# Putting the two attention products of a window back to back, with three PSUM pairs in rotation

## The chip, the cores and the metric

One core of one Trainium2 chip. The metric is the device time of one execution in microseconds (us). TensorE is called PE below, VectorE DVE, ScalarE ACT. The profiled span is about 1.8 us shorter than the device time of the same execution (284.3 against 286.09 us for the kernel before), so spans are compared with spans and times with times. The granted clock is the share of full speed at which PE was clocked. The batches of runs were on different chips, with the kernel before beside them each time.

## The reference, cut to what matters

```python
kv  = np.einsum('bhsd,bhse->bhde', k, v)          # batch 8, heads 8, seq 576, dim 64
out = np.einsum('bhsd,bhde->bhse', q, kv)
rms = np.sqrt(np.mean(out * out, axis=-1, keepdims=True) + 1e-06)
x   = (out / rms * g_norm)                         # -> 4608 tokens x 512
h   = x @ w_in                                     # 512 -> 2048
g   = np.where(h > 0.0, h, np.exp(np.minimum(h, 0.0)) - 1.0)
y   = g @ w_out                                    # 2048 -> 512
```

The 4608 tokens go in nine groups T of 512. A batch has 576 tokens, so some groups cross a batch boundary.

## The kernel before

Groups 2 to 8 run in "windows". Window T does the two layers of group T on PE, and beside it the attention of group T + 1. PSUM has eight banks of 512 floats. Pairs A and B (two banks each) take turns for the first layer, two single banks hold the output sums, and one spare pair serves the attention, one product at a time.

```python
def at_tile():
    return ps_at.tile([P, 2, 512], FP32, name="at", tag="at")
...
def se(h):                                  # half h of the attention of group T
    def product():
        st["se", h] = at_tile()
        se_mm(T, h, st["se", h])            # 16 or 24 small matmuls
        sq = attp.tile([P, 2, DM], BF16, name="sq", tag="sq")
        nc.scalar.activation(sq, st["se", h], AF.Square)
        ...
    def sums():   # DVE: ss = sum of sq over 64
    def inv():    # ACT: Ln, then Exp with scale -0.5
    def scale():  # DVE: xs = se * ss out of PSUM: frees the pair; then a DMA transpose to xT
    def gain():   # DVE: xT *= g
...
for T in range(2, NT):
    ...
    early = {2: ("sum0", "inv0"), 4: ("sum1", "inv1"), 5: ("gain0",), 7: ("gain1",)}
    late = {0: ("kv",), 1: ("se0",), 2: ("mul0",), 3: ("se1",), 4: ("mul1", "ahead")}
    ...
    halves = {1: 5, 3: 6, 5: 7} if T == 2 else {0: 1, 1: 3, 2: 4, 3: 5, 4: 6, 5: 7}
```

`early` and `late` say at which of the eight first-layer steps a piece stands, ahead of that step's DVE part or behind it; `halves` places the second layer. `kv` is K^T V of one batch, 72 small matmuls; `ahead` turns the next q by DMA and then loads the following batch. In the traces the matmuls, ACT and DVE go through their instructions in the order written. The first-layer steps have an ELU behind them: ACT takes the exponential, DVE reads the pair again and frees it.

Of the kernel before, what the change touches and what calls it, by code (L numbers as in the profile page):

```python
# [16 lines left out]
def kernel(  # L17
# [105 lines left out]
            out=w_out_sb[:, fs, :], in_=moe_w_out.rearrange("(c p) f -> p c f", p=P)[:, fs, :]  # L123
        )

    def at_tile():
        return ps_at.tile([P, 2, 512], FP32, name="at", tag="at")

    def single(tag, name):
        pool = ps_x if tag == "x" else ps_m2  # L130
        return pool.tile([P, 512], FP32, name=name, tag=tag)

    def pair(tag, name):
        if tag in ("x", "m", "mx"):
            return [single(t, name) for t in (tag + tag)[:2]]
        return ps_m1.tile([P, 2, 512], FP32, name=name, tag=tag)

    def as_bf16(ps):
# [12 lines left out]
    def kv_mm(b, kv_ps, u, ls=range(2)):  # L151
        for j in range(RK):
            for s in range(2):
                rows = slice(s * 64, s * 64 + 64)
                for l in ls:
                    nc.tensor.matmul(  # L156
                        kv_ps[s][l * 64 : l * 64 + 64, u * 64 : u * 64 + 64],
                        lhsT=bf["k", b][rows, 2 * l + u, j, :],
                        rhs=bf["v", b][rows, 2 * l + u, j, :],
                        start=(j == 0),  # L160
                        stop=(j == RK - 1),
                    )
# [78 lines left out]
    def se_mm(T, h, se_ps):  # L241

        for i in range(2):
            (b0, j0), (b1, j1) = (slot_of(T, 4 * h + 2 * i + t) for t in range(2))
            parts = [(0, P, b0, j0, 2)] if b0 == b1 else [(0, 64, b0, j0, 1), (64, P, b1, j1, 1)]
            for m in range(4):
                u, s = m // 2, m % 2
                for l in range(2):
                    for lo, hi, b, j, n in parts:
                        nc.tensor.matmul(  # L250
                            se_ps[lo:hi, l, (4 * i + m) * 64 : (4 * i + m) * 64 + 64],
                            lhsT=qT[b][l * 64 : l * 64 + 64, s, u, j : j + n, :],
                            rhs=kv_of(b, l, u, s),
                            start=True,
                            stop=True,
                        )

    def attention(T):

        st = {}  # L260

        def kv():
            if T == B:
                return
            kv_ps = at_tile()
            for u in range(2):
                kv_mm(T, [kv_ps[:, s, :] for s in range(2)], u)
            nc.scalar.copy(
                kv_sb[:, T], kv_ps[:, :, 0:P].rearrange("p s (u e) -> p u s e", u=2)
            )  # L270

        def se(h):
            def product():
                st["se", h] = at_tile()
                se_mm(T, h, st["se", h])
                sq = attp.tile([P, 2, DM], BF16, name="sq", tag="sq")
                nc.scalar.activation(sq, st["se", h], AF.Square)  # L277
                st["sq", h] = sq

            def sums():  # L280
                ss = attp.tile([P, 2 * H], FP32, name="ss", tag="ss")
                st["ss", h] = ss
                nc.vector.reduce_sum(  # L283
                    out=ss,
                    in_=st.pop(("sq", h)).rearrange("p l (m e) -> p (l m) e", e=D),
                    axis=AX.X,
                )

            def inv():
                ss = st["ss", h]  # L290
                nc.scalar.activation(ss, ss, AF.Ln, bias=eps_col, scale=1.0 / D)
                nc.scalar.activation(ss, ss, AF.Exp, scale=-0.5)  # L292

            def scale():
                if h == 0:
                    st["xs"] = attp.tile([P, J, DM], BF16, name="xs", tag="xs")
                    x_tile(T)
                se_ps, ss = st.pop(("se", h)), st.pop(("ss", h))
                nc.vector.tensor_tensor(  # L299
                    out=st["xs"][:, 2 * h : 2 * h + 2, :].rearrange("p i (l m e) -> p l i m e", l=2, e=D),  # L300
                    in0=se_ps.rearrange("p l (i m e) -> p l i m e", i=2, e=D),
                    in1=ss.rearrange("p (l i m) -> p l i m", l=2, i=2).unsqueeze(4).to_broadcast([P, 2, 2, 4, D]),
                    op=ALU.mult,
                )
                for i in (2 * h, 2 * h + 1):
                    nc.sync.dma_start_transpose(
                        out=xT[T][:, :, i * P : i * P + P], in_=st["xs"][:, i, :]
                    )

            def gain():  # L310
                cols = slice(2 * h * P, 2 * h * P + 2 * P)
                nc.vector.tensor_scalar(  # L312
                    out=xT[T][:, :, cols],
                    in0=xT[T][:, :, cols],
                    scalar1=g_col,
                    scalar2=None,
                    op0=ALU.mult,
                )

            return product, sums, inv, scale, gain  # L320

        pieces = {"kv": kv}
        for h in range(2):
            for name, piece in zip(("se", "sum", "inv", "mul", "gain"), se(h)):
                pieces[f"{name}{h}"] = piece
        return pieces

# [62 lines left out]
    def mm1(T, i, tag, relu=False):  # L390
        if i == 0:
            g_tile(T)
        ps = pair(tag, "h_ps")
        mm1_part(T, i, ps, range(KC))
        return elu(T, i, ps, relu)
# [55 lines left out]
    def mm2_half(T, i):  # L451
        mm2(T, i // 2, 8 * (i % 2), 8 * (i % 2) + 8)
# [252 lines left out]
    for i, tag in enumerate("mBAmBAm"):  # L705
        if i < 4:
            mm1(1, i, tag)()
        else:
            freed[i], rest[i] = mm1(1, i, tag, "later")
        if i == 3:  # L710
            at["kv"]()
        if i == 4:
            at["se0"]()
            freed[4]()
            at["sum0"]()
            at["inv0"]()
        if i == 5:
            at["mul0"]()
            freed[5]()
        if i == 6:  # L720
            rest[4]()
            rest[5]()
    ps = pair("B", "h_ps")
    mm1_part(1, 7, ps, range(KC))
    at["se1"]()
    freed[7], rest[7] = elu(1, 7, ps, "later")
    at["sum1"]()
    at["inv1"]()
# [22 lines left out]



    def window(T, at, early, late, second, relu=(), opened=()):
        for i in range(8):
            if i < len(opened):
                mm1_part(T, i, opened[i], range(KC), slice(256, 512))
                rest = elu(T, i, opened[i], False)
            else:
                rest = mm1(T, i, "BA"[i % 2], i in relu)  # L760
            for name in early.get(i, ()):
                at[name]()
            if i in second:
                second[i]()
            rest()
            for name in late.get(i, ()):
                at[name]()

    for T in range(2, NT):
        at, early, late = {}, {}, {}  # L770
        if T + 1 < NT:
            at = attention(T + 1)
            if T + 2 < B:
                cast_q(T + 2)

                def ahead(b=T + 2):
                    turn_q(b)
                    if b + 1 < B:
                        after_turn(b)
                        fetch_ahead(b + 1)  # L780
                at["ahead"] = ahead
            else:
                at["ahead"] = lambda: None
            early = {2: ("sum0", "inv0"), 4: ("sum1", "inv1"), 5: ("gain0",), 7: ("gain1",)}
            late = {0: ("kv",), 1: ("se0",), 2: ("mul0",), 3: ("se1",), 4: ("mul1", "ahead")}
        if T == 2:
            early = {2: ("sum0", "inv0"), 5: ("sum1", "inv1", "mul1"), 6: ("gain0",), 7: ("gain1",)}
            late = {0: ("kv",), 1: ("se0",), 2: ("mul0",), 4: ("se1",), 5: ("ahead",)}
        halves = {1: 5, 3: 6, 5: 7} if T == 2 else {0: 1, 1: 3, 2: 4, 3: 5, 4: 6, 5: 7}
        second = {i: (lambda n=n: mm2_half(T - 1, n)) for i, n in halves.items()}  # L790
        if T > 2:
            window(T, at, early, late, second)
        else:
            g_tile(T)
            opened = [pair("B", "h_ps")]
            mm1_part(T, 0, opened[0], range(KC), slice(0, 256))
            window(T, at, early, late, second, (3, 5), opened)
        mm2_half(T, 0)
        mm2_half(T, 2)
    for i in (1, 3, 4, 5):  # L800
        mm2_half(NT - 1, i)
    last_columns()
# [30 lines left out]
```

## Time and profile before

| | before |
|---|---|
| device time, median (range) of 4 runs | 285.66 us (285.14 to 285.82) |
| span of the profiled run | 284.3 us |
| PE, DVE, ACT busy | 97%, 58%, 50% |
| blocks of small matmuls in the windows | 17 |

A busy PE of 97% does not by itself say that PE can go no faster, because ends of matmuls are modelled. What says it is the distance between starts: 216 ns for every dense matmul of 512 columns. Anything that makes a start-to-start distance longer than that is what can be saved, or lost.

### The profile page before, as it was taken

What the parts mean: (1) busy time and instruction counts of PE and PEld (TensorE: products, weight loads), DVE (VectorE), ACT (ScalarE), POOL (GpSimd) and SP (SyncE); (2) the same over time, 40 slices, a digit from 0 to 9 for tenths busy, and PEclk for the clock granted to TensorE, in tenths of its full rate; (3) what the DMA queues carried; (4) which work ended last, traced back from release to release, by engine and by line L of the source; (5) the groups of instructions that cost most, each with busy time, mean ns of one, the idle gap of its engine ahead of it and who ended that gap; (6) DMA issues with size and microseconds to landing.
All of it is one profiled execution on the core that took longest, in us unless ns stands there. A gap on an engine that the chain in (4) does not pass through costs nothing.

```text
span 284.3 us, 5120 instructions
## 1 busy us (share of the span) xinstructions
PE 274.6 (97%) x2089; PEld 129.1 (45%) x2123; DVE 164.8 (58%) x222; ACT 141.5 (50%) x209; POOL 49.9 (18%) x89
## 2 busy tenths in 40 slices
PE   7899999999899999999999999999999999999994
PEld 3434444444544444444444444444444444444443
DVE  3449532877567657754785378627863786344600
ACT  3778359594568255435542555345543554333311
POOL 7743303341034033032103210000000000000000
PEclk9999999999999999999999999999999999999999
DMA  7999999997999889679637971712150234020222
GB/s 209 193 204 206 205 260 240 202 246 113 184 273 145 165 204 226 83 173 264 149 37 173 256 165 34 157 37 74 39 111 0 74 39 111 0 76 0 74 74 75
DMA packets 50571, 39.46 MB, mean 139 GB/s; under 512 B 30964, under 2 KB 44020, under 8 KB 50548
## 3 DMA queue, kind: packets, MB, share of 16 engines
q0 software_dynamic: 15008, 21.30, 37.4%
q1 hardware_dynamic: 35136, 17.31, 29.5%
q10 hardware_dynamic: 404, 0.53, 0.5%
q8 instruction: 16, 0.26, 0.4%
q14 instruction: 7, 0.06, 0.1%
HBM read 36.70 MB, written 9.44 MB: 162 GB/s over the span
## 4 chain that ended last, share of the span: by engine, by line
PE 84%; DMA 7%; DVE 3%; SPq 2%; issue 1%; ACT 1%; POOL 0%; DVEq 0%; POOLq 0%
PE h_ps L382 39%; PE o_ps L403 39%; DMA w_in_sb<-in_moe_w_in_dram 3%; DMA v_bf<-in_v_dram 2%; DMA qT<-q_bf 2%; PE at L250 2%; PE at L156 1%; PE o_ps L440 1%; PE h_ps L569 1%; DVE xs L299 1%; DVE ss L283 1%; SPq L331 1%; DVE gT L366 1%; DVE elu_e L362 1%; PE qt_ps L174 0%
## 5 line engine op out<-in xcount | busy, mean ns | idle before, releaser
L403 PE MATMUL o_ps<-w_out_sb,gT 128*128 128x512 bf16 x548 | 128.5, 379 | 0.7 <-issue 0.2
L382 PE MATMUL h_ps<-xT,w_in_sb 128*128 128x512 bf16 (+1 forms) x540 | 126.4, 376 | 1.0
L350 ACT ACTIVATE elu_e<-h_ps 128x1024 bf16<-128x1024 f32 (+1 forms) x79 | 74.0, 952 | 89.6 <-PE h_ps L382 78.4
L403 PEld LDWEIGHTS <-gT 128*128 128x128 bf16 x560 | 54.3, 98 | 66.0 <-issue 0.9
L366 DVE TENSOR_TENSOR gT<-elu_e,h_ps 128x1024 bf16<-128x1024 bf16 (+1 forms) x67 | 77.2, 1157 | 6.9 <-PE h_ps L382 0.5
L382 PEld LDWEIGHTS <-w_in_sb 128*128 128x128 bf16 x560 | 53.2, 98 | 61.1 <-issue 0.2
L362 DVE TENSOR_SCALAR elu_e<-elu_e 128x1024 bf16<-128x1024 bf16 x72 | 31.4, 437 | 65.1 <-ACT elu_e L350 65.0
L419 ACT COPY o_sb<-o_ps 128x512 f32<-128x512 f32 x32 | 18.3, 587 | 20.8 <-PE o_ps L403 20.1
L103 POOL CAST q_bf<-st_q 128x384 bf16<-128x384 f32 x36 | 18.5, 557 | 37.6 <-DMA st_q<-in_q_dram 37.6
L283 DVE TENSOR_REDUCE ss<-sq 128x16 f32<-128x1024 bf16 x14 | 17.1, 1218 | 7.7 <-ACT sq L277 7.7
L299 DVE TENSOR_TENSOR xs<-at,ss 128x1024 bf16<-128x1024 f32 x14 | 17.1, 1219 | 1.9 <-ACT ss L292 1.9
L277 ACT ACTIVATE sq<-at 128x1024 bf16<-128x1024 f32 x14 | 14.4, 1029 | 1.1 <-PE at L250 1.1
L212 DVE SCALAR_TENSOR_TENSOR xT<-y_ps,g_col,rT 128x512 bf16<-128x512 f32 (+1 forms) x10 | 6.2, 641 | 10.2 <-ACT rT L209 7.9
L339 POOL COPY gate<-qT 1x16 bf16<-1x16 bf16 x5 | 1.1, 218 | 60.4 <-DMA qT<-q_bf 60.4
L355 ACT ACTIVATE elu_h<-h_ps 128x1024 bf16<-128x1024 f32 (+1 forms) x12 | 9.3, 817 | 0.0
L156 PEld LDWEIGHTS <-k_bf 64*64 64x64 bf16 x576 | 6.4, 107 | 5.4 <-issue 5.4
L90 POOL DMA_DIRECT2D v_bf<-in_v_dram x11 | 7.8, 708 | 4.2 <-DMA w_in_sb<-in_moe_w_in_dram 2.1
L90 POOL DMA_DIRECT2D k_bf<-in_k_dram x11 | 7.9, 718 | 3.1 <-DMA w_in_sb<-in_moe_w_in_dram 2.4
L312 DVE TENSOR_SCALAR xT<-xT,g_col 128x1024 bf16<-128x1024 bf16 x14 | 6.7, 480 | 1.9 <-DMA xT<-xs 1.9
L250 PEld LDWEIGHTS <-qT 64*128 64x128 bf16 (+1 forms) x248 | 4.5, 97 | 7.1 <-issue 5.9
L250 PE MATMUL at<-kv_sb,qT 64*128 64x64 bf16 (+1 forms) x248 | 6.5, 193 | 0.8 <-DMA qT<-q_bf 0.7
L366 DVE TENSOR_TENSOR gT<-elu_e,elu_h 128x1024 bf16<-128x1024 bf16 x9 | 6.5, 723 | 0.8
(57 smaller groups left out, 94.8 us busy)
## 6 DMA issues: line engine op xcount, KB each, us to landing
st_q<-in_q_dram POOLq DMA_DIRECT2D x6, 1152.0 KB, 8.1
out_dram<-o_sb SPq DMA_DIRECT2D x24, 256.0 KB, 3.4
k_bf<-in_k_dram POOLq DMA_DIRECT2D x6, 576.0 KB, 10.6
v_bf<-in_v_dram POOLq DMA_DIRECT2D x6, 576.0 KB, 13.3
out_dram<-o_sb SPq DMA_DIRECT2D x19, 128.0 KB, 2.4
w_out_sb<-in_moe_w_out_dram POOLq DMA_DIRECT2D x4, 512.0 KB, 15.0
w_in_sb<-in_moe_w_in_dram POOLq DMA_DIRECT2D x2, 512.0 KB, 11.2
q_bf<-in_q_dram POOLq DMA_DIRECT2D x3, 288.0 KB, 13.4
```

Of the source, the lines that this page charges most:

```text
L90: eng.dma_start(out=dst.rearrange("p m j d -> p m (j d)"), in_=in_[:, ms, :])
L103: nc.gpsimd.tensor_copy(out=bf["q", b][:, u, js], in_=raw[b][:, u::2, js, :].rearrange("p l j d -> p j l d"),)
L250: nc.tensor.matmul(se_ps[lo:hi, l, (4 * i + m) * 64 : (4 * i + m) * 64 + 64], lhsT=qT[b][l * 64 : l * 64 + 64, s, u, j : j + n, :], rhs=kv ...
L277: nc.scalar.activation(sq, st["se", h], AF.Square)
L283: nc.vector.reduce_sum(out=ss, in_=st.pop(("sq", h)).rearrange("p l (m e) -> p (l m) e", e=D), axis=AX.X,)
L299: nc.vector.tensor_tensor(out=st["xs"][:, 2 * h : 2 * h + 2, :].rearrange("p i (l m e) -> p l i m e", l=2, e=D), in0=se_ps.rearrange("p l ...
L350: nc.scalar.activation(e[:, lo:hi, :], h, AF.Exp)
L362: nc.vector.tensor_scalar(out=e, in0=e, scalar1=1.0, scalar2=1.0, op0=ALU.min, op1=ALU.subtract)
L366: nc.vector.tensor_tensor(out=gT[T][:, 2 * i + lo : 2 * i + hi, :], in0=e[:, lo:hi, :], in1=h, op=ALU.add if relu else ALU.max,)
L382: nc.tensor.matmul((ps[a] if isinstance(ps, list) else ps[:, a, :])[:, cols], lhsT=w_in_sb[:, c, f * P : f * P + P], rhs=xT[T][:, c, cols] ...
L403: nc.tensor.matmul(o_ps[T, j], lhsT=gT[T][:, f, j * P : j * P + P], rhs=w_out_sb[:, f, :], start=(f == 0), stop=(f == FC - 1),)
L419: nc.scalar.copy(o_sb[T, half][:, j % 2, :], o_ps[T, j])
```

## The change

The two products of group T + 1 stand back to back, in pairs C (the spare one) and B, and in two windows K^T V of a later batch follows at once in pair A. That leaves fewer places where PE goes from the dense 128 x 128 array to smaller tiles and back. All three pairs then rotate through the first layer. A window becomes a string of steps.

```diff
+        if tag == "C":
+            return ps_at.tile([P, 2, 512], FP32, name=name, tag="at")
...
+            elif kind == "X":
+                nxt["se0"]("C")
+                nxt["se1"]("B")
+                kv_out_ = kv_all(int(arg[0]), arg[1]) if arg else None
+                if kv_out_:
+                    kv_out_()
+                for name in ("sq0", "sq1", "sum0", "sum1", "inv0", "inv1"):
+                    nxt[name]()
+            elif step == "Y":
+                nxt["mul0"]()
+                nxt["mul1"]()
...
         if T == 2:
+            window(T, "M0B K3C E0 M1A H5 E1 M2B E2 R3A H6 E3 X Y H7 Q M4A E4 h0 R5C E5 M6A E6 G0 M7B G1 E7 h2")
+        elif T + 1 < NT:
+            first = "K%dC" % (T + 1) if T < 5 else ""
+            kv = "%dA" % (T + 2) if T in (4, 5) else ""
+            window(
+                T,
+                f"M0A {first} H1 E0 M1B H3 E1 M2A H4 E2 H5 X{kv} H6 Y Q M3A H7 E3 M4B E4 M5A E5 M6C E6 G0 M7B G1 E7 h0 h2",
+            )
```

M4B is first-layer step 4 into pair B (R: with the relu on ACT), E its DVE part, H and h an eighth of the second layer for the group before or this one, K K^T V, Q the `ahead` piece, G a gain.

More of the change, by code (lines that the diff above doesn't have):

```diff
@@ L124, in load_w_out @@
         )
-    def at_tile():
-        return ps_at.tile([P, 2, 512], FP32, name="at", tag="at")
     def single(tag, name):
@@ L256, in se_mm, with kv_all, product, square @@
                         )
+    def kv_all(b, tag):
+        kv_ps = pair(tag, "kv_ps")
+        for u in range(2):
+            kv_mm(b, [kv_ps[:, s, :] for s in range(2)], u)
+        return lambda: nc.scalar.copy(
+            kv_sb[:, b], kv_ps[:, :, 0:P].rearrange("p s (u e) -> p u s e", u=2)
+        )
     def attention(T):
         st = {}
-        def kv():
-            if T == B:
-                return
-            kv_ps = at_tile()
-            for u in range(2):
-                kv_mm(T, [kv_ps[:, s, :] for s in range(2)], u)
-            nc.scalar.copy(
-                kv_sb[:, T], kv_ps[:, :, 0:P].rearrange("p s (u e) -> p u s e", u=2)
-            )
         def se(h):
-            def product():
-                st["se", h] = at_tile()
+            def product(tag="C"):
+                st["se", h] = pair(tag, "se_ps")
                 se_mm(T, h, st["se", h])
+            def square():
                 sq = attp.tile([P, 2, DM], BF16, name="sq", tag="sq")
@@ L318, in gain @@
                 )
-            return product, sums, inv, scale, gain
-        pieces = {"kv": kv}
+            return product, square, sums, inv, scale, gain
+        pieces = {}
         for h in range(2):
-            for name, piece in zip(("se", "sum", "inv", "mul", "gain"), se(h)):
+            for name, piece in zip(("se", "sq", "sum", "inv", "mul", "gain"), se(h)):
                 pieces[f"{name}{h}"] = piece
@@ L710 @@
         if i == 3:
-            at["kv"]()
+            kv_all(2, "C")()
         if i == 4:
             at["se0"]()
+            at["sq0"]()
             freed[4]()
@@ L725 @@
     at["se1"]()
+    at["sq1"]()
     freed[7], rest[7] = elu(1, 7, ps, "later")
@@ L750 @@
     at["gain1"]()
-    def window(T, at, early, late, second, relu=(), opened=()):
-        for i in range(8):
-            if i < len(opened):
-                mm1_part(T, i, opened[i], range(KC), slice(256, 512))
-                rest = elu(T, i, opened[i], False)
-            else:
-                rest = mm1(T, i, "BA"[i % 2], i in relu)
-            for name in early.get(i, ()):
-                at[name]()
-            if i in second:
-                second[i]()
-            rest()
-            for name in late.get(i, ()):
-                at[name]()
@@ L769 @@
-    for T in range(2, NT):
-        at, early, late = {}, {}, {}
-        if T + 1 < NT:
-            at = attention(T + 1)
-            if T + 2 < B:
-                cast_q(T + 2)
-                def ahead(b=T + 2):
-                    turn_q(b)
-                    if b + 1 < B:
-                        after_turn(b)
-                        fetch_ahead(b + 1)
-                at["ahead"] = ahead
-            else:
-                at["ahead"] = lambda: None
-            early = {2: ("sum0", "inv0"), 4: ("sum1", "inv1"), 5: ("gain0",), 7: ("gain1",)}
-            late = {0: ("kv",), 1: ("se0",), 2: ("mul0",), 3: ("se1",), 4: ("mul1", "ahead")}
-        if T == 2:
-            early = {2: ("sum0", "inv0"), 5: ("sum1", "inv1", "mul1"), 6: ("gain0",), 7: ("gain1",)}
-            late = {0: ("kv",), 1: ("se0",), 2: ("mul0",), 4: ("se1",), 5: ("ahead",)}
-        halves = {1: 5, 3: 6, 5: 7} if T == 2 else {0: 1, 1: 3, 2: 4, 3: 5, 4: 6, 5: 7}
-        second = {i: (lambda n=n: mm2_half(T - 1, n)) for i, n in halves.items()}
-        if T > 2:
-            window(T, at, early, late, second)
-        else:
-            g_tile(T)
-            opened = [pair("B", "h_ps")]
-            mm1_part(T, 0, opened[0], range(KC), slice(0, 256))
-            window(T, at, early, late, second, (3, 5), opened)
-        mm2_half(T, 0)
-        mm2_half(T, 2)
@@ new lines, in mm1_rest, with window @@
+    def mm1_rest(T, i, tag, relu):
+        mm1_part(T, i, opened, range(KC), slice(256, 512))
+        return elu(T, i, opened, relu)
+    def window(T, steps):
+        rest = {}
+        nxt = attention(T + 1) if T + 1 < NT else None
+        for step in steps.split():
+            kind, arg = step[0], step[1:]
+            if kind in "MR":
+                i, tag = int(arg[0]), arg[1]
+                make = mm1_rest if T == 2 and i == 0 else mm1
+                rest[i] = make(T, i, tag, kind == "R")
+            elif kind == "E":
+                rest.pop(int(arg))()
+            elif kind == "H":
+                mm2_half(T - 1, int(arg))
+            elif kind == "h":
+                mm2_half(T, int(arg))
+            elif kind == "K":
+                kv_all(int(arg[0]), arg[1])()
+            elif kind == "X":
[9 more added lines that the diff above has]
+                nxt["mul1"]()
+            elif step == "Q":
+                b = T + 2
+                if b < B:
+                    turn_q(b)
+                if b + 1 < B:
+                    after_turn(b)
+                    fetch_ahead(b + 1)
+            elif kind == "G":
+                nxt[f"gain{arg}"]()
+            else:
+                raise ValueError(step)
@@ new lines @@
+    g_tile(2)
+    opened = pair("B", "h_ps")
+    mm1_part(2, 0, opened, range(KC), slice(0, 256))
+    for T in range(2, NT):
+        if T + 2 < B:
+            cast_q(T + 2)
+        if T == 2:
+            window(T, "M0B K3C E0 M1A H5 E1 M2B E2 R3A H6 E3 X Y H7 Q M4A E4 h0 R5C E5 M6A E6 G0 M7B G1 E7 h2")
[5 more added lines that the diff above has]
+                f"M0A {first} H1 E0 M1B H3 E1 M2A H4 E2 H5 X{kv} H6 Y Q M3A H7 E3 M4B E4 M5A E5 M6C E6 G0 M7B G1 E7 h0 h2",
+            )
+        else:
+            window(T, "M0A H1 E0 M1B H3 E1 M2A H4 E2 M3B H5 E3 M4A H6 E4 M5B H7 E5 M6A E6 M7B E7 h0 h2")
```

## The prediction

> **What bounds the kernel now.** I first read the page: the engine table, the groups, the chain of waits.
>
> ```profile
> PE 274.6 (97%) x2089; PEld 129.1 (45%) x2123; DVE 164.8 (58%) x222; ACT 141.5 (50%) x209; POOL 49.9 (18%) x89
> ...
> PE 84%; DMA 7%; DVE 3%; SPq 2%; issue 1%; ACT 1%; POOL 0%; DVEq 0%; POOLq 0%
> ...
> L403 PE MATMUL o_ps<-w_out_sb,gT 128*128 128x512 bf16 x548 | 128.5, 379 | 0.7 <-issue 0.2
> L382 PE MATMUL h_ps<-xT,w_in_sb 128*128 128x512 bf16 (+1 forms) x540 | 126.4, 376 | 1.0
> L283 DVE TENSOR_REDUCE ss<-sq 128x16 f32<-128x1024 bf16 x14 | 17.1, 1218 | 7.7 <-ACT sq L277 7.7
> L299 DVE TENSOR_TENSOR xs<-at,ss 128x1024 bf16<-128x1024 f32 x14 | 17.1, 1219 | 1.9 <-ACT ss L292 1.9
> L277 ACT ACTIVATE sq<-at 128x1024 bf16<-128x1024 f32 x14 | 14.4, 1029 | 1.1 <-PE at L250 1.1
> ```
>
> PE carries 84% of the chain and sits idle under 2 us before its two dense groups. DVE and ACT are half busy. So only two things can move the time: PE work that is not dense, and a new wait of PE. Next I read PE's timeline for one steady window (start, length, line):
>
> ```profile
> 102.19 1.89 PE L403 MATMUL o_ps<-w_out_sb,gT 128*128 128x512 bf16 x8
> 104.01 0.41 PE L250 MATMUL at<-kv_sb,qT 64*128 64x64 bf16 x16
> 104.35 1.90 PE L382 MATMUL h_ps<-xT,w_in_sb 128*128 128x512 bf16 x8
> 106.09 1.89 PE L403 MATMUL o_ps<-w_out_sb,gT 128*128 128x512 bf16 x8
> ```
>
> Dense groups of 8 start 1.73 us apart: 216 ns each, no slack. An attention product of 16 small matmuls stretches 102.19 to 104.35 to 2.16 us, so it costs 0.43. Single records split that: the last dense matmul starts at 103.700 and the first small one at 104.008, 308 ns instead of 216; the small ones go in pairs every 29 ns; from the last (104.229) to the next dense one is 122 ns. So about 0.1 us to enter and 0.11 to leave, besides 8 x 0.029 = 0.23 of work. A K^T V of 72 costs 0.80 by the same subtraction (128.764 to 129.783 less 0.216). A product with a group boundary in it uses two array shapes (64*128 and 64*64): 24 matmuls, 0.57, with another 125 ns step between the shapes.
>
> The waits of PE hold one more item, in the first later window:
>
> ```profile
> PE at L250 <- DMA qT<-q_bf: 0.7, 1, 0.7
> ```
>
> The records show two pauses there (77.05 to 77.36 and 77.36 to 78.26). From the last dense start (76.517) to the next (78.475) less 0.216 is 1.74 us where such a block costs 0.57: this wait costs 1.17 us.
>
> **What the Trainium skill says.** "TensorEngine Tiling (Array Packing)", Key Properties: changing the tiling mode, not just the tile, drains the TensorE. The trace agrees: 0.1 us at each change of shape. "TensorE: Matmul & The Clock Gate", the part on 56 against 53.3 ns: N / 2.4 + about 2.5 ns, 215.7 at N = 512; the trace has 216. "VectorE: DVE Perf Modes", the perf-mode tier table: a reduce runs at 1x, and a tensor_tensor with a PSUM operand at 1x. The trace agrees: 1218 and 1219 ns for 1024 elements. So four such DVE operations in a row cannot be quick, and that matters below.
>
> **The change part by part.** No instruction is added or removed on PE (4247 rows in both); the order alone changes. In a later window M, H, E are the first layer, half of a second-layer sum, and the DVE part of ELU; X is the two products back to back (into pairs C and B), with K^T V into A behind them in two windows; Y is the two scalings.
>
> (a) Fewer mode switches. Before: 17 blocks (5 K^T V, 12 products). Cost 5 x 0.80 + 9 x 0.44 + 3 x 0.57 = 9.7 us. After: 9 blocks, 3 K^T V alone and 6 X. An X of 32 equal matmuls is 16 x 0.029 + 0.21 = 0.68; with an inner boundary 0.80; the two with K^T V (0.58 of work plus one more change) are 1.57 and 1.36. Sum 3 x 0.80 + 0.79 + 0.68 + 1.57 + 1.36 + 0.80 + 0.68 = 8.3. **Saved: 1.4 us**, all on the path, since PE has no slack.
>
> (b) The qT wait goes. In the first later window X comes after M0 to M3, H5 and H6, at about 82 us by adding dense groups from 70.7. The transpose lands at 78.2. **Saved: 1.17 us.**
>
> (c) A new wait. Pair B now holds the second product until its scaling, and M4 wants B. Put X's start at 0 in a window without K^T V in X. From the trace: after a preceding output copy on ACT, the square starts 0.68 after the block begins (104.60 against 103.92). Then square to reduce 1.06, reduces and scalings on DVE start 1.13 apart back to back (107.88 to 109.01). First reduce 1.74; second 2.87; the two Ln/Exp pairs (0.33 + 0.24 each) fall beside them, ready at 3.57 and 4.70; scaling 0 at 4.00; scaling 1 at 5.13, ending 6.35. With 0.06 for the semaphore (an estimate), B is free at 6.41. PE reaches M4 after X and three groups (H6, M3, H7): 0.68 + 3 x 1.73 = 5.87. **Wait 0.54 us.** With the inner boundary PE comes 0.12 later: 0.42. Where K^T V lies in X, its copy stands on ACT ahead of both squares: the squares start at about 1.9, not 0.68, B is free at 7.5 to 7.75, and PE arrives at 6.55 or 6.76: about 0.96 each. Sum over the five windows: 0.54 x 2 + 0.42 + 0.97 + 0.96 = **3.4 us added**. In the one-product-at-a-time order before, nothing waited for the scaling: each had the spare pair to itself.
>
> (d) The first later window uses B again only at M7. But its DVE queue does the two scalings ahead of E4, so M6 waits some 0.2 us for pair A, and the second gain (behind E6) ends some 0.3 us after PE is ready for the next window's M0. **Added: 0.5 us.**
>
> (e) K^T V of batches 6 and 7 is formed a window earlier, so k and v must land earlier. Before, v of batch 7 landed at 169.5, 44.0 us after its window's M0 (125.5). The new order issues it about 0.9 earlier; PE asks for it 43.7 after that M0 by my sum of groups. Margin about 0.6 us, for 576 KB loads that took 11.3 to 13.9 us. Batch 6 has a margin of about 2 us. **Expected: 0.2 us**, a third of a chance of a larger wait.
>
> Sum: -1.4 - 1.17 + 3.4 + 0.5 + 0.2 = +1.5 us on 285.75, that is 287.3. I take 287.0, leaning slightly to the side of the saving, because each wait in (c) is the small difference of two sums of some 6 us.
>
> **The rivals.** First: the switches and the qT wait go and no wait comes, 283.2 us. For it: the switch cost is plain in the records; an order set step by step was presumably meant to fit. Against it: DVE needs 6.35 us from X to the last scaling and PE only 5.87, and nothing in the change shortens the DVE work; the program has M4's first matmul wait on DVE. Second: the wait on pair B is there and takes back more than the saving, about 287. Third: the wait on v for batch 7 comes on top, or the early K^T V delays the window more than I count, 288 to 289. Against it: the loads are only shifted, and DMA is far from full there. A fourth, that the PE clock falls in the new waits: against it, the page grants full clock throughout, through the existing 0.9 us pause too; no change.
>
> **Range and chances.** 80% range 283.6 to 288.8: the lower end is nearly the first rival, the upper the third. Two per cent is 5.7 us. Faster by that would need more than twice the total of what is removable here; slower would need the new waits to be twice what I sum, or a long DMA wait in several windows. Both are remote.
>
> **What would show it.** In the changed profile: L250 and L156 form 9 blocks instead of 17, X of 32 matmuls lasts 0.68 from dense start to dense start less 0.216, and the two with K^T V about 1.4 to 1.6 (a). No PE wait for qT (b). The waits of PE show the first layer waiting for DVE's scaling of xs five times, 0.4 to 1.0 us each (c); if that row is missing or under 1 us in sum, (c) is wrong and the time is near 283.5. A short PE idle before M6 and before M0 of the window after the first (d). A PE wait for v_bf near 170 us would be (e). What I may have wrong: how fast ACT and DVE start behind one another, so the size of (c), and which window's load is late.

## The result, and the profile after

287.72 us median of 4 runs (287.58 to 288.56) against 285.66 us. The ratio is 1.0081, 95% interval 1.0058 to 1.0105. Here and below a ratio is the mean time of one kernel's runs over that of the other's in the same rounds, so it is not quite the ratio of the medians. The change costs 0.8%: the interval is clear of 1.

The page of the changed kernel, in the parts that were shown of the kernel before (each function stands one line earlier: L381 is the first layer, L402 the second, L282 the reduce, L298 the scaling, L276 the square):

```profile
PE 274.8 (96%) x2094; PEld 129.7 (45%) x2123; DVE 163.3 (57%) x222; ACT 142.0 (49%) x209; POOL 50.0 (17%) x89
...
PE 72%; DVE 12%; DMA 6%; ACT 4%; issue 3%; SPq 1%; POOL 1%; DVEq 0%; POOLq 0%
...
L381 PE MATMUL h_ps<-xT,w_in_sb 128*128 128x512 bf16 (+1 forms) x551 | 125.6, 376 | 3.4 <-DVE xs L298 2.6
L402 PE MATMUL o_ps<-w_out_sb,gT 128*128 128x512 bf16 x542 | 127.4, 379 | 1.3 <-issue 0.6
...
L282 DVE TENSOR_REDUCE ss<-sq 128x16 f32<-128x1024 bf16 x14 | 16.5, 1214 | 16.6 <-ACT sq L276 16.6
...
L298 DVE TENSOR_TENSOR xs<-se_ps,ss 128x1024 bf16<-128x1024 f32 x14 | 16.5, 1216 | 1.2 <-ACT ss L291 1.2
L276 ACT ACTIVATE sq<-se_ps 128x1024 bf16<-128x1024 f32 x14 | 13.7, 1029 | 0.3 <-PE se_ps L249 0.3
```

No group shown grew. What moved is the chain: DVE from 3% to 12%, ACT from 1% to 4%, PE from 84% to 72%. Square, reduce and scaling are now links in the chain that sets the end. The waits of PE, whole (us in total, times, longest):

```profile
PE h_ps L381 <- DVE xs L298: 2.6, 5, 0.8
PE kv_ps L524 <- DVE one L517: 1.2, 1, 1.2
PE kv_ps L155 <- DMA v_bf<-in_v_dram: 0.9, 1, 0.9
PE o_ps L402 <- issue: 0.6, 4, 0.2
PE y_ps L188 <- DVE kv_sb L112: 0.5, 2, 0.3
PE kv_ps L155 <- DVE kv_sb L112: 0.4, 1, 0.4
PE kv_ps L155 <- DVE v_bf L112: 0.3, 1, 0.3
PE h_ps L381 <- DVE xT L311: 0.2, 1, 0.2
PE h_ps L568 <- DVE xT L211: 0.2, 1, 0.2
```

The first and eighth rows are new, the third is 0.9 us in the middle of the windows, and the wait for qT is gone. (The issue row comes from matmuls that the trace lacks a record of; the rest is of the start.) PE's timeline of the second later window shows where the first row comes from:

```profile
104.98 3.62 PE L402 MATMUL o_ps<-w_out_sb,gT 128*128 128x512 bf16 x16
108.53 0.64 PE L249 MATMUL se_ps<-kv_sb,qT 64*128 64x64 bf16 x32
109.11 1.90 PE L402 MATMUL o_ps<-w_out_sb,gT 128*128 128x512 bf16 x7
110.84 1.89 PE L381 MATMUL h_ps<-xT,w_in_sb 128*128 128x512 bf16 x8
112.57 1.89 PE L402 MATMUL o_ps<-w_out_sb,gT 128*128 128x512 bf16 x8
114.84 7.07 PE L381 MATMUL h_ps<-xT,w_in_sb 128*128 128x512 bf16 x31 [0.38 <-DVE xs L298]
```

Both products are one block of 32, and 104.98 to 109.11 less 16 dense starts (3.45) is 0.68 us. Groups of eight follow 1.73 apart, but M4 (114.84) comes 2.27 after the group before it: a wait of 0.54. The 0.38 in brackets is less because the modelled end of a matmul covers 0.16 us of it; the same holds for each of the five waits, so the 2.6 us of the wait row are 3.35 us on the clock (0.54, 0.93, 0.93, 0.41, 0.54). DVE's timeline says what M4 waited for:

```profile
110.18 2.35 DVE L282 TENSOR_REDUCE ss<-sq 128x16 f32<-128x1024 bf16 x2 [2.16 <-ACT sq L276]
112.44 2.35 DVE L298 TENSOR_TENSOR xs<-se_ps,ss 128x1024 bf16<-128x1024 f32 x2
```

Two reduces and two scalings back to back end at 114.79, and PE starts 0.05 us later. Pair B is held until the last of the four.

### The profile page after: what moved, and what is told of

It is laid out like the page before. It is cut to its first block, busy times and chain, and to the rows that moved or that the text cites. A ratio compares the mean times of both kernels' runs of the same rounds, so it can differ in the third digit from the quotient of the medians.

```text
span 286.8 us, 5147 instructions
## 1 busy us (share of the span) xinstructions
PE 274.8 (96%) x2094; PEld 129.7 (45%) x2123; DVE 163.3 (57%) x222; ACT 142.0 (49%) x209; POOL 50.0 (17%) x89
## 4 chain that ended last, share of the span: by engine, by line
PE 72%; DVE 12%; DMA 6%; ACT 4%; issue 3%; SPq 1%; POOL 1%; DVEq 0%; POOLq 0%
PE h_ps L381 33%; PE o_ps L402 30%; DVE xs L298 5%; DMA v_bf<-in_v_dram 5%; DVE ss L282 4%; PE kv_ps L155 2%; ACT sq L276 2%; PE kv_ps L524 2%; DMA qT<-q_bf 1%; PE h_ps L568 1%; PE o_ps L439 1%; PE qt_ps L173 1%; DVE gT L365 1%; SPq L305 1%; ACT elu_e L349 1%
## 5 line engine op out<-in xcount | busy, mean ns | idle before, releaser
L381 PE MATMUL h_ps<-xT,w_in_sb 128*128 128x512 bf16 (+1 forms) x551 | 125.6, 376 | 3.4 <-DVE xs L298 2.6
L402 PE MATMUL o_ps<-w_out_sb,gT 128*128 128x512 bf16 x542 | 127.4, 379 | 1.3 <-issue 0.6
L381 PEld LDWEIGHTS <-w_in_sb 128*128 128x128 bf16 x560 | 54.4, 98 | 68.2 <-issue 4.5
L402 PEld LDWEIGHTS <-gT 128*128 128x128 bf16 x560 | 53.7, 98 | 64.3 <-issue 0.9
L282 DVE TENSOR_REDUCE ss<-sq 128x16 f32<-128x1024 bf16 x14 | 16.5, 1214 | 16.6 <-ACT sq L276 16.6
L298 DVE TENSOR_TENSOR xs<-se_ps,ss 128x1024 bf16<-128x1024 f32 x14 | 16.5, 1216 | 1.2 <-ACT ss L291 1.2
L276 ACT ACTIVATE sq<-se_ps 128x1024 bf16<-128x1024 f32 x14 | 13.7, 1029 | 0.3 <-PE se_ps L249 0.3
L155 PE MATMUL kv_ps<-v_bf,k_bf 64*64 64x64 bf16 x576 | 7.5, 194 | 1.5 <-DMA v_bf<-in_v_dram 0.9
L290 ACT ACTIVATE ss<-ss,eps_col 128x16 f32<-128x16 f32 x14 | 4.3, 308 | 6.4 <-DVE ss L282 6.4
```

Source lines behind the costliest of these rows:

```text
L155: nc.tensor.matmul(kv_ps[s][l * 64 : l * 64 + 64, u * 64 : u * 64 + 64], lhsT=bf["k", b][rows, 2 * l + u, j, :], rhs=bf["v", b][rows, 2 * ...
L282: nc.vector.reduce_sum(out=ss, in_=st.pop(("sq", h)).rearrange("p l (m e) -> p (l m) e", e=D), axis=AX.X,)
L298: nc.vector.tensor_tensor(out=st["xs"][:, 2 * h : 2 * h + 2, :].rearrange("p i (l m e) -> p l i m e", l=2, e=D), in0=se_ps.rearrange("p l ...
L381: nc.tensor.matmul((ps[a] if isinstance(ps, list) else ps[:, a, :])[:, cols], lhsT=w_in_sb[:, c, f * P : f * P + P], rhs=xT[T][:, c, cols] ...
L402: nc.tensor.matmul(o_ps[T, j], lhsT=gT[T][:, f, j * P : j * P + P], rhs=w_out_sb[:, f, :], start=(f == 0), stop=(f == FC - 1),)
```

## The experiments

The theory: the grouping saves what was predicted, and the loss is PE waiting for pair B, with a smaller wait for v of batch 7. Rivals: the mode switches saved were worth nothing; the grouped order loses in another place, with these waits only its shadow; or the first window carries it all. In each batch of runs the kernel before was run beside them: 285.83 us (first four experiments), 285.67 (next three), 285.87 (last three).

| run | median us | ratio to before, 95% interval |
|---|---|---|
| changed kernel | 287.72 | 1.0081 [1.0058, 1.0105] |
| rotate | 287.29 (286.1 to 290.32) | 1.0064 [1.0015, 1.0112] |
| kv_later | 286.96 | 1.0038 [1.0026, 1.0050] |
| both | 284.56 | 0.9956 [0.9944, 0.9969] |
| reduce_twice | 295.72 (294.0 to 297.36) | 1.0345 [1.0311, 1.0380] |
| split | 285.45 | 0.9992 [0.9978, 1.0006] |
| first_only | 285.51 | 0.9993 [0.9981, 1.0006] |
| first_window_too | 283.85 | 0.9937 [0.9925, 0.9950] |
| kv6_early | 283.76 | 0.9925 [0.9912, 0.9939] |

All ten experiment runs gave correct results.

### rotate: M4 takes the pair that is free

The part of the window's line that differs:

```diff
-H7 E3 M4B E4 M5A E5 M6C E6 G0 M7B G1
+H7 E3 M4C E4 M5B E5 M6A E6 G0 M7C G1
```

> The changed kernel with one edit: in the later windows M4 takes pair C, M5 pair B, M6 pair A, M7 pair C (it was B, A, C, B). Theory (the wait on pair B): C is free about 1.1 us before B, so all five waits of the first layer on the scaling go (3.3 us in the changed kernel), but the load of v for batch 7 does not come earlier while PE asks for it 0.93 us earlier (the wait of the window before it is gone), so the v wait grows from 0.9 to about 1.8 us. Sum: 287.7 - 3.3 + 0.9 = 285.3 us. If a general slowdown of the grouped order is the cause and not the pair, the time stays near 287.7.

The five waits on the scaling are gone from the waits of PE, and the wait on v became 1.9 us of idle time, as forecast (1.8):

```profile
167.23 0.64 PE L249 MATMUL se_ps<-kv_sb,qT 64*128 64x64 bf16 x32
169.80 0.77 PE L155 MATMUL kv_ps<-v_bf,k_bf 64*64 64x64 bf16 x72 [1.93 <-DMA v_bf<-in_v_dram]
170.51 2.87 PE L402 MATMUL o_ps<-w_out_sb,gT 128*128 128x512 bf16 x7
```

Yet no run came down to the 285.3 us of the forecast, and the profiled run was hardly shorter than the changed kernel (span 286.5 against 286.8). The stretches of the trace around the v wait tell why. The columns are length; busy time and count of PE, weight loads, DVE, ACT, POOL; granted PE clock; DMA share; GB/s:

```profile
165.00:170.00 5.00, 3.07 (x68) 1.61 (x70) 1.76 (x2) 0.59 (x1) 0.91 (x2) 1.00 0.89 197
170.00:172.00 2.00, 1.95 (x76) 1.12 (x66) 0.03 (x1) 1.36 (x3) 0.00 (x0) 0.82 0.04 8
172.00:174.00 2.00, 2.00 (x6) 0.63 (x5) 2.00 (x2) 1.38 (x3) 0.00 (x0) 0.50 0.00 0
174.00:176.00 2.00, 2.00 (x9) 0.88 (x8) 2.00 (x3) 0.66 (x3) 0.00 (x0) 0.83 0.00 0
176.00:178.00 2.00, 2.00 (x11) 0.87 (x9) 1.56 (x3) 1.30 (x2) 0.00 (x0) 1.00 0.33 67
```

After the wait the clock is granted at one half; the clock record in the trace lasts 3.41 us. PE is shown busy throughout, but 6 matmuls touch the stretch at half clock where 11 touch the one at full clock. Half of 3.41 us, 1.7 us, is lost; by starts too, the three groups from 170.51 to 177.38 take 6.87 us in place of 5.18. That is a second price of a wait. It is not paid each time: in reduce_twice, below, PE idles for 2.02 and 2.03 us and keeps its clock.

The changes of clock in this trace are whole multiples of 3.413 us apart (49, then 1, then 33). In the step of that length ahead of the drop (167.87 to 171.28) PE was busy for 42% by the profile. A step of reduce_twice (145.0 to 148.42) was also busy for 42%, with dense matmuls alone where this one has the 72 small ones, and no drop followed. What decides between the two is not shown.

The six runs fall apart: 286.1, 286.26 and 286.3 at a mean clock of 0.997 to 0.999, and 288.29, 289.28 and 290.32 at 0.993 to 0.994. Only one of the long ones has a trace. The mean clocks of the other two allow for a loss of up to about 1.7 us each (an estimate, 0.006 of 288 us), as in the traced one, but they are 3 and 4 us longer than the short runs: something more is in them, which no trace shows. So the pair rotation alone moves the wait to the load of v, as said, with the clock as a new cost, and the median of this run is that of a mixture.

### kv_later: no K^T V inside X

```diff
-first = "K%dC" % (T + 1) if T < 5 else ""
-kv = "%dA" % (T + 2) if T in (4, 5) else ""
+first = "K%dC" % (T + 1) if T < 7 else ""
+kv = ""
```

> The changed kernel with one edit: no K^T V inside X; batches 6 and 7 get theirs behind M0 of the windows where the kernel before had them. Theory: the v wait goes (-0.9), ACT no longer copies K^T V ahead of the squares so two waits on pair B fall from 0.93 each to 0.42 and 0.54 (-0.9), and two more blocks cost 2 x 0.11 = +0.2. Sum about 286.1 us. If the early K^T V is what pays for the change, as its author meant, it gets slower than 287.7.

286.96 us, 0.8 us less than the changed kernel, not 1.6. In the trace everything forecast is there: no wait on v, and waits on the scaling of 0.55, 0.31, 0.54, 0.41 and 0.54 us, 1.0 less in sum than 3.35. The forecast was too good because it took 0.93 us of v wait from the first profile, which was the slowest of the four runs of the changed kernel (288.56; the others 287.6 to 287.8). By profile, the gain is 286.79 to 285.05 in span, 1.7 us, as forecast; by median, 0.8 (0.9 when each is taken less the kernel before of its own batch). The second look at the changed kernel, below, shows how that wait varies.

### both: the two edits together

> Both edits: rotation C, B, A, C and K^T V later. Theory: no wait on pair B and none on v: 287.7 - 3.3 - 0.9 + 0.2 = 283.7 us, that is 2 us under the kernel before, which is the mode switches and the qT wait saved less the 0.65 of the first later window. If the switches saved are worth nothing, it lands at 285.0 (the qT wait and the first window alone).

284.56 us, 1.3 us under the kernel before and not 2: the forecast, 283.7, again took 0.9 us for the wait on v from a median whose runs have little of it. Without that, 287.72 - 3.35 + 0.2 gives 284.57. The first six rows of the waits of PE:

```profile
PE kv_ps L524 <- DVE one L517: 1.2, 1, 1.2
PE o_ps L402 <- issue: 1.0, 6, 0.2
PE y_ps L188 <- DVE kv_sb L112: 0.5, 2, 0.3
PE kv_ps L155 <- DVE v_bf L112: 0.5, 1, 0.5
PE kv_ps L155 <- DVE kv_sb L112: 0.4, 1, 0.4
PE h_ps L381 <- DVE xT L311: 0.2, 1, 0.2
```

Neither the scaling nor v of batch 7 is there; the kv_ps rows are of the start, before the windows, and the last row is the wait of M0 behind the first window. DVE does exactly what it did, two reduces and two scalings in a row, but PE no longer asks for what they hold:

```profile
110.71 1.89 PE L381 MATMUL h_ps<-xT,w_in_sb 128*128 128x512 bf16 x8
112.44 1.89 PE L402 MATMUL o_ps<-w_out_sb,gT 128*128 128x512 bf16 x8
114.17 4.05 PE L381 MATMUL h_ps<-xT,w_in_sb 128*128 128x512 bf16 x18
```

M4 starts 1.73 us after the group before it, without a wait. Taking away these waits, and nothing else but two blocks put back, turned a loss of 0.8% into a gain of 0.4%. The sharpest comparison is with kv_later, which ran in the same batch and differs from this kernel in the rotation alone: 286.96 - 284.56 is 2.40 us, and its five waits on the scaling are 2.35 us in sum. What the grouping loses besides is the 0.65 us of the first later window (below).

### reduce_twice: DVE made slower on purpose

```diff
-nc.vector.reduce_sum(out=ss, in_=st.pop(("sq", h))...)
+for _ in range(2 if T >= 4 and h == 1 else 1):
+    nc.vector.reduce_sum(out=ss, in_=sq...)
```

> The changed kernel with the second reduce of each later group (five groups) done twice, the same values: 1.13 us more on DVE before the scalings, nothing on PE. Theory: PE waits for the scaling, so each of the five waits on pair B grows by 1.13 us: 287.7 + 5.6 = 293.3 us. If DVE is not on PE's path there, DVE at 57% takes it up and the time stays near 287.7.

```profile
112.67 1.89 PE L404 MATMUL o_ps<-w_out_sb,gT 128*128 128x512 bf16 x8
116.19 7.07 PE L383 MATMUL h_ps<-xT,w_in_sb 128*128 128x512 bf16 x31 [1.64 <-DVE xs L300]
```

The waits of M4 became 1.80, 2.19, 2.19, 1.67 and 1.80 us, each 1.26 more than in the changed kernel (1.13 was forecast); one reduce lasts 1.21. The v wait vanished, since PE now asks later. The profiled run took 294.0 us, where 293.3 was forecast. The other three took 295.57 to 297.36, with mean clocks of 0.988 to 0.992: they have no trace, but the drop is the size of one or two stretches of 3.4 us at half clock. So a DVE that is busy 57% of the time sits on the path here, because PE waits for the end of one particular row of DVE operations.

### split: the switches alone

The kernel of "both", with one dense group of 8 put between the two products of five windows (the part of the line that differs):

```diff
-H4 E2 H5 X H6 Y Q M3A
+H4 E2 S0C H5 S1B U0 U1 H6 V0 V1 Q M3A
```

> The kernel of the run named both, with one edit: in the five windows from the second on, the first product is moved ahead of H5, so that one dense group of 8 lies between the two products; pairs and all else as there, and no wait is added by my sums. Theory (each block pays an entry and a leave, about 0.21 us together): 5 x 0.21 = 1.05 us slower than both. If switches cost nothing on the path, it equals both.

0.9992 against 0.9956 of the kernel before: 0.0036 of 285.7 is 1.0 us for five blocks, 0.21 us a block, with an uncertainty of about half of that from the two intervals. The traces say it more closely: by starts, the two separate products cost 0.20 us more than the pair in four windows and 0.10 in one, where splitting them also takes away a step between two small shapes; 0.9 us in sum. No wait on the scaling is in its trace. (In its profiled run the first later window was also held up once for 0.5 us by the gain before it, ahead of the part that was edited.) The switch saving is real, and 0.20 us a block is nearly the predicted 0.21.

### first_only: the new order in the first later window alone

Windows after it in the old order, with pair C for the spare pair:

```diff
+f"M0A H1 E0 {kv} M1B H3 E1 S0C M2A U0 H4 E2 V0 M3B H5 E3 S1C M4A U1 H6 E4 V1 Q M5B G0 H7 E5 M6A E6 M7B G1 E7 h0 h2"
```

> The changed order in the first later window alone; the windows after it in the order of the kernel before, with pair C in the place of the spare pair. Theory: the qT wait (1.17) and one block (0.1 net of an inner boundary) are saved, the waits before M6 (0.25) and before the next M0 (0.40) are added: 285.7 - 0.6 = 285.1 us. If the first window carries the whole saving of the change, it should come near 283.5.

285.51 us, 0.9993 with an interval that includes 1: this window is worth some 0.2 us, which is not told apart from nothing, and not 0.6. Its trace has the two waits that were forecast, 0.24 us before M6's pair is free and 0.41 us before the next M0. What was smaller was the saving (see the second look at the kernel before, below). So the first window does not carry the change.

### first_window_too: that window mended as well

The kernel of "both", with h2 ahead of M6, both gains ahead of E6, and the next M0 on pair C:

```diff
-h0 R5C E5 M6A E6 G0 M7B G1 E7 h2
+h0 R5C E5 h2 M6A G0 G1 E6 M7B E7
...
-f"M0A {first} H1 E0 ..."                     # the window after it, T == 3
+f"M0C {first} H1 E0 ..."                     # with first = "K4A"
```

> The kernel of the run named both, with the first later window mended as well: h2 ahead of M6, both gains ahead of E6, and the next window's M0 on pair C, its K^T V on A. Theory: the waits before M6 and before the next M0 (0.65 us) go: 283.7 - 0.65 = 283.0 us. If those were shadows of something else, it equals both.

283.85 us, 0.9937: 0.5 us (by the ratios) to 0.7 us (by the medians) under "both", where 0.65 was forecast; the intervals of the two ratios just overlap. In its trace no dense matmul of the windows starts late, so both waits are gone. The level that was forecast, 283.0, is missed by what the forecast of "both" was missed by.

### A second look at both kernels, and K^T V of batch 6

> The kernel before, looked at a second time. The first profile has a span of 284.3 us, while its timed runs of 285.66 us stand for spans near 283.9. Theory: what varies is the wait for qT in the first later window (1.17 us in the first profile): here it is shorter by some 0.4 us. If it is 1.17 again, the 0.4 us lies elsewhere, in the start.

> The changed kernel, looked at a second time. Its profiled run is 0.9 us longer than its three timed ones (288.56 against 287.6 to 287.8). Theory: the wait on v of batch 7 (0.93 us in the first profile) varies from run to run with the load, and a run of 287.6 us has next to none; the five waits on the scaling stay 0.4 to 0.9 each, 3.3 to 3.4 us in sum.

In the second profile of the kernel before (285.62 us) the wait for qT shows as

```profile
PE at L250 <- DMA qT<-q_bf: 0.5, 1, 0.5
```

By starts, the block costs 1.26 us here against 0.57 for such a block without a wait: 0.69 of wait, where the first profile had 1.17. The 0.4 us are in that wait. That is what first_only and the prediction had taken too large.

The changed kernel, looked at again, took 288.06 us. The waits for the scaling were 0.55, 0.93, 0.94, 0.41 and 0.54 us, the same to 0.01. The wait for v was 0.45 us instead of 0.93: the load landed 11.9 us after its issue, not 13.5, but it was also issued 1.1 us later (at 157.31, not 156.24). I had expected next to none, but this run was not one of 287.6 us, so that the fast ones have none remains an inference from their times.

Why v is issued no earlier than before shows in SyncE's queue, first of the kernel before and then of the changed one (first profiles):

```profile
139.63 9.95 SPq L306 DMA_TRANSPOSE xT<-xs  x4
149.67 2.81 SPq L331 DMA_TRANSPOSE qT<-q_bf  x2
...
144.68 5.15 SPq L305 DMA_TRANSPOSE xT<-xs  x4
149.92 3.15 SPq L330 DMA_TRANSPOSE qT<-q_bf  x2
```

The last scaling of that window ends 0.93 us earlier after M0 than before. But the four DMA transposes of xs, which the kernel before issued two at a time, now stand in a row of 5.15 us. The turn of q stands behind them and starts 0.58 us later after M0 than before. The loads stand behind the turn of q: the copy on POOL that waits for it starts 3.6 us after it in the kernel before, 4.0 and 5.1 us in the two profiles of the changed one. So from M0 to the issue of v it is 30.15 us before, 31.04 and 32.14 after. Why the turn of q took longer is not shown.

The last run puts K^T V of batch 6 back behind the two products of the window before:

```diff
-first = "K%d%s" % (T + 1, "A" if T == 3 else "C") if T < 7 else ""
-kv = ""
+first = "K%d%s" % (T + 1, "A" if T == 3 else "C") if T in (3, 4, 6) else ""
+kv = "6A" if T == 4 else ""
```

> The kernel of the run named first_window_too, with K^T V of batch 6 back inside X of the window before, behind the two products; batch 7 stays late. Theory: v of batch 6 lands 1.9 us before PE asks for it, so no wait, and one block less saves 0.11 us; ACT then copies K^T V ahead of the squares, but C is free 0.1 to 0.2 us before M4 in that window by my sums. So 0.1 us under first_window_too (0.9937 of the kernel before), at the edge of what can be told. If pair C comes free too late there, it is up to 0.3 us slower.

283.76 us, 0.9925 [0.9912, 0.9939]: with first_window_too (0.9937) it cannot be told apart at these intervals. Neither has a wait on v of batch 6 or 7. These two beat both the kernel before and the changed one.

## Why the prediction was right, point by point

It said 287.0 us within 283.6 to 288.8, and 287.72 was measured. By its own parts:

- **(a) Fewer switches, -1.4 us: mechanism right, size slightly large.** By starts, and without the waits in them, the blocks of the windows cost 9.6 us before and 8.4 after, 1.2 saved. A block of 32 took 0.67 (0.68 was said) and the one with K^T V of batch 6 1.61 (1.57). The one in the first later window took 0.91, not 0.79: its group boundary lies in the middle, which makes two steps between small shapes and not one.
- **(b) The qT wait, -1.17 us: mechanism right, size too large.** It was taken from a single profile; the second one has 0.69.
- **(c) The wait on pair B, +3.4 us: held.** 3.35 us, and each of the five within 0.04 of its forecast. Rotating the pairs removed it, lengthening DVE's row by 1.2 us lengthened each wait by 1.26.
- **(d) The first window, +0.5 us: slightly small.** 0.24 before M6 (0.2 was said) and 0.41 before M0 (0.3).
- **(e) v of batch 7, +0.2 us: the wait came, by a step that was wrong.** PE would have asked for v 43.7 us after M0, as predicted, and the loads took 13.5 and 11.9 us, within the 11.3 to 13.9 that it gave. But it had v issued 0.9 us earlier after M0 than before, and v was issued 0.9 and 2.0 us later, behind the row of transposes of xs and a slower turn of q (above). The waits were 0.93 and 0.45 us in the two profiles; that 0.2 is near what the timed runs have, by their times, is luck.
- **The sum.** The measured terms, -1.2 - 0.7 + 3.35 + 0.65, are +2.1 us with no wait on v; the medians differ by 2.06. With the v wait and the qT wait of each profile they give 2.6 twice, where the spans differ by 2.5 and 2.4. So the terms leave next to nothing over. Of the +1.5 of the prediction, (a), (b) and (d) had 0.8 us too little, and the lean from 287.3 to 287.0 went the wrong way as well.

Of the rivals, the first (no wait, 283.2) is what the repaired order reaches, 283.8. The third (v on top, 288 to 289) is what the two profiled runs of the changed kernel show, 288.56 and 288.06; its three other runs do not. The fourth (the clock falls in the waits) was put aside on the ground of one pause of 0.9 us. That held for the changed kernel, but not always with waits twice as long, as rotate showed.

## What to carry to other kernels

Grouping work to save array-mode switches also groups its consumers. Here four DVE operations stand in a row, and a first-layer step that wants the second pair cannot start before the last of them has ended; four transposes stand in a row too, and later loads wait behind them. When buffers rotate, write down when each will be free, and give the next step the one that is free first. A wait of PE costs its own length, and in one trace here nearly as much again in clock (1.7 us behind an idle time of 1.93).

## What the Trainium skill lacked or had wrong

- "TensorEngine Tiling (Array Packing)", Key Properties, says that a mode switch drains the TensorE but has no number: here 0.09 us to enter, 0.11 to leave, and 0.20 us by starts for each of four blocks put back between dense matmuls (split).
- "TensorE: Matmul & The Clock Gate", the closing table, advises no PE-idle gaps over about 3 us. Here an idle time of 1.93 us, with small matmuls of 0.6 and 0.8 us on either side, was followed by 3.41 us at half clock (rotate), which cost 1.7 us; five idle times of 1.5 to 2.0 us in the profiled run of reduce_twice were not, while its other runs show a lower mean clock. Its 3413 ns window agrees with the length of the drop. Its part on a second failure mode names frequent short idles between groups of matmuls in another kernel; that a single idle time of 1.93 us can be enough, it does not say, and the runs here do not show when it is.
- "DMA: Bandwidth & Descriptors", Anatomy of one DMA, fits 2.0 us plus bytes over 436 GB/s, an estimate of 3.4 us for the 576 KB of v by itself. It gives no figure for a load behind others: as the third of three loads issued together, v landed 11.9 and 13.5 us after issue in the two profiles of the changed kernel.
